# Eight single PSUM banks, gathered tails of M, and a new order in a two-block kernel

## The chip, the cores and the metric

The kernel runs on one core of one Trainium2 chip. A core has several engines with an instruction list each: TensorE (PE, matmuls, with its weight loads shown as PEld), VectorE (DVE), ScalarE (ACT), GpSimd (POOL) and SyncE (SP), which here issues all DMAs. An engine takes its own list in order and waits for others through semaphores. PE writes to PSUM alone, and DVE and ACT take results out of it ("evict" them) into SBUF.

The metric is the time of one launch on the device in microseconds (us), lower is better. The span of a profile is the time from the first to the last instruction; the launch's own time is a little longer.

## The reference

Two blocks that share nothing are computed and set side by side in the last dimension. Block A is a long convolution over the sequence (S = 2048, D = 576) by FFT, with a short convolution and gates around it. Block B is linear attention with 32 heads of 18 columns.

```python
# A: k_shift = sum over 4 taps of k_pad[:, t:t+S] * shift_k;  kv = k_shift * v
kv_f = rfft(kv_pad);  kf_f = rfft(kf_pad)          # length 2 * S
y = irfft(kv_f * kf_f)[:S].astype(bf16)
a = q * (y + kv * ssm_D)

# B: q, k, v = split of x @ wqkv into 32 heads of 18 columns
phi = lambda t: where(t > 0, t + 1, exp(t)) + 1e-6
kv = einsum("bhsd,bhse->bhde", phi(k), v);  z = einsum("bhsd->bhd", phi(k))
num = einsum("bhqd,bhde->bhqe", phi(q), kv)
den = einsum("bhqd,bhd->bhq", phi(q), z)[..., None] + 1e-6
b = (num / den) merged @ wo

out = concatenate([a, b], axis=-1)
```

## The kernel before

Every piece of work is a small function, called a unit, and the string ORDER lists the units one after another. A scheduler is not at work: each engine gets its instructions in the order in which the units are written. A unit's name is followed by its arguments, by letters that say which engine does its vector work (A for ACT, D for DVE, P for POOL, N for "not done, the matmuls of the next stage take both summands"), and after a slash by digits that name the buffers it takes.

Block A's 576 channels go in five chunks: four of 128 and one of 64. For each chunk the filter (h) and the gated input (u) pass the same stages:

- hT turns the filter's rows (on PE, or through a copy and a transposing DMA), and cv makes u by the short convolution in at, one multiply and one multiply-add pair per tap.
- h1 and u1 (L536) are the first half of the transform: matmuls with the matrix G, evicted into Ch and Cu. G is computed in the kernel by index arithmetic on DVE (ix) and a sine on ACT (sin).
- ht and ut transpose Ch and Cu by DMA into Cth and Ctu (L543), each in two halves.
- h2 and u2 (L559) are the second half, evicted into T and SU.
- pX and pT multiply SU with T into X and T, pA and pS add or subtract their two planes.
- i1 (L593) and i2 (L606, L607) are the inverse; i2 reads F, the transposed G, which FT makes by a transposing DMA (L613), and multiplies its result into q.

Block B computes k and q (k, q, qt; L455, L464) with an exponential on ACT and a combination on DVE (phi). It forms G = x' * phi(k) (L661), kv from it and the weights of v, M = kv * wo (b_M, L712 to L719), the denominators (den), their reciprocals, and bc and bt, which spread the reciprocals over the heads and multiply them into phi(q) (pqT and pq4). The output units o and ol multiply pqT and pq4 by M (L783, L775) and send the rows out.

PSUM is given out in four slots of two banks each: a unit's tile takes a whole slot, however small it is. M has 576 columns, more than a bank holds in 32-bit numbers, so each of M's five units makes 512 columns and then 64, evicted together. The denominators' unit also makes a column that carries the epsilon (ez) in the same slot.

The two memsets that set the bias row of the weights wqk (one_w, unit wm) stand behind the first evictions on DVE.

## Time and profile before

| What | us |
|---|---|
| launch, median of 3 runs | 161.46 |
| launch, lowest and highest of the 3 | 159.47, 189.46 |
| launch of the profiled execution | 159.33 |
| its span | 157.6 |

Mean granted PE clock over the profiled execution: 0.989 of full speed. Section 2 of the page cuts the span into 40 slices; each digit is the busy share of a slice in tenths:

```profile
PE   7999999999998999999999999999899999999991
DVE  6989779898999699997999998999998998899810
ACT  4999999999987899959999757998997969796141
POOL 6048703709113963008100049289998050230000
PEclk9999999999999999999999999999987999999999
```

PE is at nine tenths or more in nearly every slice, DVE and ACT in most. In a row of the timeline the columns are the start, the duration, the engine, the line, the operation with what it writes and reads, and in brackets how long the engine was idle before it and what ended that.

### The profile page before, as it was taken

The page shows a single profiled execution, that of the slowest core. Times are in us where ns is not written, and L with a number is a line of the kernel's source. Part 1 is how long each engine was busy: PE and PEld are TensorE (multiplying, and loading weights), DVE is VectorE, ACT ScalarE, POOL GpSimd, SP SyncE. Part 2 cuts the span into 40 slices and gives each one's busy share as a digit, 9 for nine tenths or more (in the row PEclk, how much of TensorE's full clock was granted, in tenths as well). Part 3 has the DMA queues.
Part 4 walks back from the last instruction along what each step waited for, and adds up shares of the span by engine and source line. Part 5 has one row for each costly group of instructions (what it writes and reads, how often), then busy time and mean ns, then how long its engine had stood idle before and what let it go on. Part 6 is the DMA issues. An engine that isn't in the chain of part 4 may idle for free.

```text
span 157.6 us, 4600 instructions
## 1 busy us (share of the span) xinstructions
PE 149.6 (95%) x1986; PEld 90.3 (57%) x1986; DVE 135.8 (86%) x169; ACT 130.5 (83%) x162; POOL 62.0 (39%) x70
## 2 busy tenths in 40 slices
PE   7999999999998999999999999999899999999991
PEld 2686555467533467367566468585445565578650
DVE  6989779898999699997999998999998998899810
ACT  4999999999987899959999757998997969796141
POOL 6048703709113963008100049289998050230000
PEclk9999999999999999999999999999987999999999
DMA  3986999999999699999999787697987999636076
GB/s 86 391 282 188 294 300 186 253 290 266 184 186 225 127 317 264 143 213 324 177 176 176 209 109 144 192 141 146 263 170 148 131 319 186 173 107 189 0 227 198
DMA packets 74315, 31.92 MB, mean 203 GB/s; under 512 B 52090, under 2 KB 73653, under 8 KB 74294
## 3 DMA queue, kind: packets, MB, share of 16 engines
q1 hardware_dynamic: 74294, 31.62, 91.5%
q8 instruction: 15, 0.25, 0.6%
q14 instruction: 6, 0.05, 0.1%
HBM read 14.97 MB, written 4.72 MB: 125 GB/s over the span
## 4 chain that ended last, share of the span: by engine, by line
PE 77%; ACT 12%; DMA 3%; DVE 3%; issue 1%; POOL 1%; DVEq 0%; POOLq 0%; ACTq 0%
PE k_ps L455 12%; PE g_ps L661 10%; PE o_ps L783 9%; PE s_ps L536 8%; PE q_ps L464 8%; PE i_ps L593 6%; PE s_ps L559 5%; DMA Ctu<-Cu 3%; PE i_ps L606 3%; PE i_ps L607 2%; ACT V L308 2%; ACT T L308 2%; ACT Cu L308 2%; PE o_ps L775 2%; ACT G L231 2%; PE qt_ps L472 2%
## 5 line engine op out<-in xcount | busy, mean ns | idle before, releaser
L455 PE MATMUL k_ps<-wqk,xT 128*128 128x512 bf16 (+1 forms) x160 | 21.5, 286 | 0.0
L536 PEld LDWEIGHTS <-G 128*128 128x128 bf16 x320 | 17.4, 98 | 3.6 <-issue 2.7
L464 PE MATMUL q_ps<-xT,wqk 128*128 128x512 bf16 x80 | 18.4, 380 | 0.0
L308 ACT ACTIVATE Cu<-s_ps 128x1024 bf16<-128x1024 f32 (+1 forms) x18 | 17.0, 976 | 0.4 <-PE s_ps L536 0.2
L455 PEld LDWEIGHTS <-xT 128*128 128x128 bf16 x160 | 11.4, 98 | 10.5 <-issue 0.3
L308 ACT ACTIVATE T<-s_ps 128x1024 bf16<-128x1024 f32 x17 | 16.8, 1026 | 0.6 <-PE s_ps L559 0.6
L308 ACT ACTIVATE ob<-o_ps 128x576 bf16<-128x576 f32 (+1 forms) x15 | 9.2, 637 | 9.1 <-PE o_ps L775 4.8
L661 PE MATMUL g_ps<-pk,x_sb 128*128 128x512 bf16 (+1 forms) x128 | 16.5, 286 | 0.0
L308 ACT ACTIVATE Ch<-s_ps 128x1024 bf16<-128x1024 f32 (+1 forms) x17 | 15.2, 928 | 1.0 <-PE s_ps L536 1.0
L494 DVE TENSOR_TENSOR at<-at 128x2048 bf16<-128x2048 bf16 (+1 forms) x14 | 15.5, 1109 | 0.5
L308 ACT ACTIVATE SU<-s_ps 128x1024 bf16<-128x1024 f32 x15 | 15.0, 1040 | 1.0 <-PE s_ps L559 1.0
L308 ACT ACTIVATE V<-i_ps 128x1024 bf16<-128x1024 f32 x15 | 14.7, 1039 | 1.0 <-PE i_ps L593 1.0
L783 PE MATMUL o_ps<-wo_M,pqT 128*128 128x512 bf16 (+1 forms) x112 | 14.9, 286 | 0.0
L448 DVE SCALAR_TENSOR_TENSOR pk<-pk,k_ps 128x576 bf16<-128x576 bf16 x16 | 11.8, 751 | 3.4 <-ACT pk L447 3.3
L493 DVE TENSOR_TENSOR at<-k,Wj 128x2048 bf16<-128x2048 bf16 (+1 forms) x13 | 14.7, 1134 | 0.1
L661 PEld LDWEIGHTS <-x_sb 128*128 128x128 bf16 x128 | 8.4, 97 | 8.9 <-issue 1.2
L447 ACT ACTIVATE pk<-k_ps,neg 128x576 bf16<-128x576 f32 x16 | 11.6, 741 | 1.3 <-PE k_ps L455 0.9
L464 PEld LDWEIGHTS <-wqk 128*128 128x128 bf16 x80 | 7.4, 98 | 9.1 <-issue 1.3
L608 DVE TENSOR_TENSOR q<-i_ps,q 128x1024 bf16<-128x1024 f32 (+1 forms) x10 | 10.9, 1105 | 1.9 <-PE i_ps L607 1.8
L783 PEld LDWEIGHTS <-pqT 128*128 128x128 bf16 x112 | 7.5, 98 | 7.7 <-issue 0.9
L536 PE MATMUL s_ps<-hT,G 128*128 128x128 bf16 (+1 forms) x160 | 10.7, 216 | 1.0 <-ACT G L231 0.4
L593 PE MATMUL i_ps<-W,T 64*128 64x128 bf16 x160 | 11.3, 217 | 0.4 <-DVE pqT L753 0.4
(163 smaller groups left out, 336.0 us busy)
## 6 DMA issues: line engine op xcount, KB each, us to landing
x_sb<-in_B_x_dram SPq DMA_DIRECT2D x4, 576.0 KB, 6.6
h_sb<-in_A_ssm_k_dram SPq DMA_DIRECT2D x4, 512.0 KB, 6.1
out_dram<-ob SPq DMA_DIRECT2D x7, 288.0 KB, 5.3
k<-in_A_k_dram SPq DMA_DIRECT2D x1, 1280.0 KB
v<-in_A_v_dram SPq DMA_DIRECT2D x1, 1280.0 KB
q<-in_A_q_dram SPq DMA_DIRECT2D x1, 1280.0 KB
wqk<-in_B_wqkv_dram SPq DMA_DIRECT2D x2, 576.0 KB, 7.8
k<-in_A_k_dram SPq DMA_DIRECT2D x1, 1024.0 KB
```

Source lines behind the costliest of these rows:

```text
L308: nc.scalar.activation(out=out, in_=in_, func=ACT.Copy)
L447: nc.scalar.activation(out=out_ap, in_=ps_ap, func=ACT.Exp, bias=K.neg1[0:n, :])
L448: nc.vector.scalar_tensor_tensor(out=out_ap, in0=out_ap, scalar=1.0, in1=ps_ap, op0=ALU.min, op1=ALU.max)
L455: nc.tensor.matmul(ps[:, n0:n1], lhsT=xT[r // 4][:, t, rr * 128:(rr + 1) * 128], rhs=wqk[:, t, D + n0:D + n1], start=(t == 0), stop=(t == 4))
L464: nc.tensor.matmul(ps[:, j, :], lhsT=wqk[:, t, 128 * c:128 * c + 128], rhs=xT[g][:, t, :], start=(t == 0), stop=(t == 4))
L493: on[0].tensor_tensor(out=t_, in0=kk[:, 3 - stage:19 - stage], in1=wb(stage), op=ALU.mult)
L494: on[1].tensor_tensor(out=a_, in0=a_, in1=t_, op=ALU.add)
L536: nc.tensor.matmul(ps[:, bi, 0:dc], lhsT=K.G[ri][:, b, :], rhs=xf(b), start=True, stop=True)
L593: nc.tensor.matmul(ps[:, r, g, :], lhsT=s[key, hf][64 * r:64 * r + 64, z, x, 128 * g:128 * g + 128], rhs=K.W[64 * r:64 * r + 64, m, :], st ...
L608: nc.vector.tensor_tensor(out=qs, in0=ps[:, :, 0:dc], in1=qs, op=ALU.mult)
L661: nc.tensor.matmul(ps[:, n0:n1], lhsT=x_sb[:, r, f0:f0 + fn], rhs=pk[:, r, n0:n1], start=(r == 0), stop=(r == 15))
L783: nc.tensor.matmul(pss[i][:, n0:n1], lhsT=pqT[:, c, r * 128:(r + 1) * 128], rhs=B['M'][:, c, n0:n1], start=(c == 0 and not first), stop=(c ...
```

## The change

PSUM becomes one tile of eight banks of 512 32-bit columns, and the digits in the order name a bank; a tile takes the banks that its size needs, from that one on. The tiles of the last, narrow chunk are made as wide as they are, so that they fit one bank.

M is split: b_M makes 512 columns in one bank, and a new unit Mt makes the 64 last columns of all five parts in another, with one eviction. The epsilon column of the denominators gets a unit of its own, ez, in a bank of its own, right behind zz.

```diff
+    allps = pspool.tile([128, 4096], FP32, name="allps")
     class Banks:
         def tile(self, shape, dt, name):
-            return pspool.tile(shape, dt, name=name, tag="ps" + slots.pop(0))
+            o = 512 * int(slots.pop(0))
+            v = allps[:, o:o + n // 2].bitcast(BF) if dt == BF else allps[:, o:o + n]
...
-        ps = psum.tile([128, 8, 128], FP32, name="s1_ps")
+        ps = psum.tile([128, 8, dc], FP32, name="s1_ps")
...
+    def m_mul(ps, c, n0, n1):
+        h0, hn = HCH[c]
+        if c < 4:
+            nc.tensor.matmul(ps, lhsT=B['kvT'][0:hn, c, :], rhs=B['wo'][0:hn, c, n0:n1], start=True, stop=False)
+            m = HCH[c + 1][1]
+            nc.tensor.matmul(ps, lhsT=B['kvx'][0:m, c, :], rhs=B['wo'][0:m, c + 1, n0:n1], start=False, stop=True)
...
     def b_M(c, eng='A'):
-        ps = psum.tile([128, 1024], FP32, name="m_ps")
-        for n0, n1 in ((0, 512), (512, 576)):
...
-        evict(B['M'][:, c, :], ps[:, 0:D], eng)
+        ps = psum.tile([128, 512], FP32, name="m_ps")
+        m_mul(ps[:], c, 0, 512)
+        evict(B['M'][:, c, 0:512], ps[:], eng)
+
+    def b_Mt(eng='A'):
+        ps = psum.tile([128, 5, 64], FP32, name="m_ps")
+        for c in range(5):
+            m_mul(ps[:, c, :], c, 512, 576)
+        evict(B['M'][:, :, 512:576], ps[:], eng)
+
+    def b_ez():
+        ps = psum.tile([128, 2], FP32, name="ez_ps")
...
+        ez = B['ez'] = ab.tile([128, 1], FP32, name="ez")
+        nc.vector.tensor_scalar_add(out=ez[:], in0=ps[:, 0:1], scalar1=EPS)
...
     def b_den():
-        ps = psum.tile([128, 1024], FP32, name="den_ps")
+        ps = psum.tile([128, 512], FP32, name="den_ps")
...
-        ez = ab.tile([128, 1], FP32, name="ez")
-        nc.vector.tensor_scalar_add(out=ez[:], in0=ps[:, 512:513], scalar1=EPS)
-        den = ps[:, 0:512]
+        ez = B['ez']
+        den = ps[:]
...
-io ls ix.0.0/0 sin.1.0 wu.1.A/0 wu.2.B/1 dl ix.1.0/1 sin.0.0 hl.0/0 dc/2 hd.0 Wj.A/301 ix.0.1 id xl.2 iw ix.1.1 sin.0.1
+io wm wu.1.A/0 ix.0.0/0 xl.2 sin.1.0 wu.2.B/1 dl ix.1.0/1 sin.0.0 dc/2 ls ix.0.1 ix.1.1 id sin.1.1 hl.0/0 hd.0 iw
```

Apart from that the whole order is new. Most units stay near their place; some change engine. In the rows below a name left of the arrow is what is written, and behind it what is read; in the changed kernel every PSUM tile reads as allps, and line numbers are ten to twenty higher.

At the head of DVE's list before (sm holds small constants, mp and mc the indices of the sines):

```order
L135 MEMSET epsc 128x1
L381 MEMSET sm 1x64
L148 TENSOR_SCALAR sm<-sm 128x128
L150 TENSOR_SCALAR mp<-sm 128x128
L153 TENSOR_TENSOR mp<-mp,sm 128x128
```

and in the changed kernel, at the same place:

```order
L135 MEMSET epsc 128x1
L371 MEMSET wqk 64x576
L372 MEMSET wqk 1x576
L148 TENSOR_SCALAR sm<-sm 128x128
L150 TENSOR_SCALAR mp<-sm 128x128
```

The two memsets of wqk have moved ahead of the first index operation.

DVE between kv and the last product of pqT before (Ch, SU, T are evictions or products of block A, at the short convolution, Gz holds the reciprocals):

```order
L310 CAST SU<-s_ps 128x2x512
L573 TENSOR_TENSOR T<-SU,T 128x2048
L493 TENSOR_TENSOR at<-k,Wj 128x16x64
L494 TENSOR_TENSOR at<-at 128x16x64
L739 TENSOR_SCALAR ez<-den_ps 128x1
L741 TENSOR_SCALAR den_ps<-den_ps,ez 128x512
L743 RECIPROCAL Gz<-den_ps 128x512
L608 TENSOR_TENSOR q<-i_ps,q 128x8x128 x2
L753 SCALAR_TENSOR_TENSOR pqT<-pqT,bc_ps 128x1024 x2
L762 SCALAR_TENSOR_TENSOR pq_77<-pq_77,bt_ps 128x1024
L310 CAST T<-s_ps 128x2x512
L753 SCALAR_TENSOR_TENSOR pqT<-pqT,bc_ps 128x1024 x6
```

and in the changed kernel:

```order
L320 CAST SU<-allps 128x2x512
L501 TENSOR_TENSOR at<-k,Wj 128x16x64
L583 TENSOR_TENSOR T<-SU,T 128x2048
L761 TENSOR_SCALAR allps<-allps,ez 128x512
L763 RECIPROCAL Gz<-allps 128x512
L618 TENSOR_TENSOR q<-allps,q 128x8x128 x2
L773 SCALAR_TENSOR_TENSOR pqT<-pqT,allps 128x1024 x2
L782 SCALAR_TENSOR_TENSOR pq_78<-pq_78,allps 128x1024
L773 SCALAR_TENSOR_TENSOR pqT<-pqT,allps 128x1024 x2
L320 CAST Ch<-allps 128x2x16x16
L773 SCALAR_TENSOR_TENSOR pqT<-pqT,allps 128x1024 x4
```

A multiply and an add of the convolution, the eviction of T and ez have left this stretch; the first step of the last convolution and a half-width Ch have come into it.

SP's queue around the transposes of F before:

```order
L543 DMA_TRANSPOSE Cth<-Ch 128x16x128 x2
L613 DMA_TRANSPOSE F_1350<-G_107 128x16x128
L524 DMA_TRANSPOSE hT<-hp 128x16x128
L632 DMA wv_GT<-in_B_wqkv_dram 128x4x576
L634 DMA wv_GT<-in_B_wqkv_dram 64x576 x2
L543 DMA_TRANSPOSE Ctu<-Cu 128x16x128 x2
L646 DMA wo_M<-in_B_wo_dram 126x4x576
```

and in the changed kernel:

```order
L642 DMA wv_GT<-in_B_wqkv_dram 128x4x576
L644 DMA wv_GT<-in_B_wqkv_dram 64x576 x2
L553 DMA_TRANSPOSE Cth<-Ch 128x16x128 x2
L534 DMA_TRANSPOSE hT<-hp 128x16x128
L623 DMA_TRANSPOSE F_1509<-G_126 128x16x128
L623 DMA_TRANSPOSE F_1511<-G_114 128x16x128
L553 DMA_TRANSPOSE Ctu<-Cu 128x16x128 x2
L656 DMA wo_M<-in_B_wo_dram 126x4x576
```

Both transposes of F now stand behind hT and right ahead of Ctu; one of them came from a place between the first two Ctu transposes, much earlier, and the loads of the weights of v have moved ahead of Cth.

## The prediction

> **What bounds the kernel now.** I read the page's busy times first, then the two stretches into which the trace divides around 122 us, then the timelines of the engines where PE (TensorE) loses time. In the windows the columns are busy time and instruction count of PE, PEld, DVE, ACT and POOL, then granted clock, DMA share and GB/s.

> ```profile
> span 157.6 us, 4600 instructions
> PE 149.6 (95%) x1986; PEld 90.3 (57%) x1986; DVE 135.8 (86%) x169; ACT 130.5 (83%) x162; POOL 62.0 (39%) x70
> 98.00:122.00 24.00, 22.26 (x404) 13.58 (x405) 23.02 (x22) 22.07 (x29) 20.02 (x7) 0.93 0.86 175
> 122.00:154.00 32.00, 31.76 (x475) 19.57 (x469) 25.77 (x29) 21.90 (x30) 4.25 (x2) 1.00 0.71 168
> 114.00:116.00 2.00, 1.68 (x34) 1.07 (x32) 2.00 (x3) 2.00 (x4) 2.00 (x2) 1.00 0.81 161
> 116.00:118.00 2.00, 1.98 (x25) 0.90 (x18) 2.00 (x3) 1.84 (x3) 2.00 (x2) 0.71 0.95 196
> 118.00:120.00 2.00, 2.00 (x24) 0.66 (x22) 1.31 (x2) 1.25 (x3) 2.00 (x2) 0.50 1.11 210
> 120.00:122.00 2.00, 1.64 (x60) 1.31 (x46) 2.00 (x3) 1.83 (x3) 1.38 (x1) 0.94 0.43 84
> ```

> PE is the bound: 149.6 of 157.6 us, and 31.76 of the last 32 us before the final output. A kernel that does the same matmuls can win only what PE loses. The largest loss stands between 98 and 122 us: 24.00 - 22.26 = 1.74 us idle, and a clock that fell to 0.71, 0.50 and 0.94, which costs 2 x (0.29 + 0.50 + 0.06) = 1.70 us of matmul rate. There DVE (VectorE) is busy for 23.02 of 24 us, more than PE. So in this stretch, the only one, I take DVE's list of work as what sets the pace; behind it PE does.

> The change keeps the matmuls of M, of the denominators and of everything else, moves them, and gives PSUM out in single banks. I go through it by the places where it touches a bound.

> **Start.** The memset pair that prepares wqk moves from its place among the evictions to the head of DVE's list, ahead of the index arithmetic on which the first sine waits.

> ```profile
> 1.28 0.29 DVE L148 TENSOR_SCALAR sm<-sm 128x128 int32<-128x128 f32 x1 [0.17 <-POOL sm L121]
> 5.41 0.28 DVE L69 TENSOR_SCALAR ident<-sm 128x128 bf16<-128x128 f32 x1
> 12.53 0.54 DVE L361 MEMSET wqk<- 64x576 int32 x1
> 13.71 0.57 DVE L207 TENSOR_SCALAR sm<-sm 128x448 int32<-128x448 int32 x1
> 3.62 1.15 ACT L231 ACTIVATE G<-mp,negpi 128x1024 bf16<-128x1024 int16 x1 [1.32 <-DVE sm L427]
> 4.00:8.00 4.00, 3.91 (x45) 2.62 (x44) 3.72 (x11) 3.97 (x7) 0.00 (x0) 1.00 1.05 392
> 8.00:12.00 4.00, 3.63 (x61) 3.35 (x59) 3.36 (x4) 4.00 (x8) 1.79 (x5) 1.00 0.78 267
> ```

> From the first of the pair (L361) to the row behind the second (L207) are 13.71 - 12.53 = 1.18 us. DVE would start it at about 1.0 us and come to L148 at 2.18 instead of 1.28: +0.9 us. The first sine, which waited 1.32 us for DVE, starts 0.9 us later, and ACT (ScalarE) has no slack to take it back: 3.97 of 4 and 4.00 of 4 us. The identity moves behind the second half of the indices too, to about 7.2 us, so PE's first transposes come later, but those wait for ACT's evictions in any case. I take +1.0 us on the first k matmuls. Bounds: 0 if ACT loses its small waits, +1.5 if PE's start follows the identity in full (7.2 - 5.41 = 1.8, less PE's wait for the sine).

> **The two DMA waits near 45 us.** PE waits twice there for a transposed copy of stage-one results.

> ```profile
> 42.01 0.62 PE L559 MATMUL s_ps<-Cth,W 64*32 64x512 bf16 x16 [0.34 <-DMA Cth<-Ch]
> 48.24 0.41 PE L559 MATMUL s_ps<-Ctu,W 64*32 64x512 bf16 x8 [0.52 <-DMA Ctu<-Cu]
> 43.02 2.17 SPq L543 DMA_TRANSPOSE Ctu<-Cu  x1
> 45.23 2.53 SPq L613 DMA_TRANSPOSE F<-G  x1
> 47.86 2.62 SPq L543 DMA_TRANSPOSE Ctu<-Cu  x1
> ```

> Together 0.86 us. SP's queue, not PE, sets when these land, and the same loads stand ahead of them, so a PE that comes 1.0 us later finds them there; besides, the 2.53 us transpose of F leaves the place between the two Ctu transposes. I take -0.8 (bounds -0.86 and 0, if SP slips as much as PE). Start and DMA waits together: +0.2. What is late next on SP is F itself; that is a rival below.

> **Extra matmuls.** One sum of two planes after another is left to the matmuls of the inverse stage (N in the order): pA of chunk 0, half 0 gets its addition on DVE (16 matmuls fewer), pS of chunk 1, half 1 and of chunk 2, half 0 lose theirs (32 more). Net 16.

> ```profile
> 72.59 2.12 PE i_ps L593 x72
> ```

> 2.12 / 72 = 29 ns each, so 0.47 us of PE. They add in full if PE is the bound where they stand; the second 16 stand just ahead of the output rows, at a place where PE waits for DVE now. I take +0.1 of it beyond that cover.

> **DVE between the denominators and the first output rows.** The first output unit starts when the last product of pqT and the spread reciprocals is done.

> ```profile
> 101.56 0.68 DVE L493 TENSOR_TENSOR at<-k,Wj 128x1024 bf16<-128x1024 bf16 x1
> 102.28 0.69 DVE L494 TENSOR_TENSOR at<-at 128x1024 bf16<-128x1024 bf16 x1
> 102.89 0.15 DVE L739 TENSOR_SCALAR ez<-den_ps 128x1 f32<-128x1 f32 x1
> 103.94 3.36 DVE L743 RECIPROCAL Gz<-den_ps 128x512 bf16<-128x512 f32 x1
> 113.01 1.23 DVE L310 CAST T<-s_ps 128x1024 bf16<-128x1024 f32 x1
> 119.51 2.35 DVE L753 SCALAR_TENSOR_TENSOR pqT<-pqT,bc_ps 128x1024 bf16<-128x1024 bf16 x2 [0.69 <-PE bc_ps L749]
> 93.07 0.68 DVE L491 TENSOR_TENSOR at<-k,Wj 128x1024 bf16<-128x1024 bf16 x1
> 127.97 0.69 DVE L310 CAST Cu<-s_ps 128x512 bf16<-128x512 f32 x1 [0.34 <-PE s_ps L536]
> 122.49 2.13 PE L783 MATMUL o_ps<-wo_M,pqT 128*128 128x512 bf16 x16
> ```

> From this list go the two convolution steps of the last chunk, to POOL (0.68 + 0.69), the eviction of one T, to ACT (1.23, whose successors start 1.14 after it), and ez (0.15), which moves to the place after zsel: -2.6. To it come the first convolution step (0.68, seen at 93.07) and one half-width Ch eviction (0.69 by the like eviction of Cu): +1.3. Net -1.3 us. The last products now start at 119.51 and end at 121.86, and PE's first long output matmuls stand at 122.49. The 0.69 us for which DVE waits on bc_ps falls in the slow-clock time; I give half of it, 0.3, to the finer banks: M, den, ez and the half-width tiles hold one bank and not two, so bc finds a free pair sooner. That makes -1.6. Bounds of this term: 0, if PE and not DVE sets the pace, and -3.4, if all idle time and all clock loss (1.74 + 1.70) go.

> POOL's cover: its queue has the two convolution steps (2.14 us each by POOL's own convolution row) in the 3.3 us that it waits for SU now, and gets rid of three X sums. If they came late, the next to wait would be X and T of chunk 2 and then the inverse stage, behind POOL's 20.02 of 24 us.

> ```profile
> 117.16 2.14 POOL L493 TENSOR_TENSOR at<-k,Wj 128x1024 bf16<-128x1024 bf16 x1
> 102.89 4.06 POOL L571 TENSOR_TENSOR X<-SU,T 128x2048 bf16<-128x2048 bf16 x1 [3.28 <-ACT SU L308]
> 105.35 1.24 ACT L308 ACTIVATE wo_M<-m_ps 128x576 bf16<-128x576 f32 x2
> ```

> The tails of M: five evictions of 576 columns become five of 512 and one of 320. At 0.62 us each, and nearly the same per column, ACT gains or loses some 0.3 us of fixed cost; ACT idles 24.00 - 22.07 = 1.93 us there. I take 0, bounds 0 and +0.3.

> [...] By the three rows, time at half clock was 1.70 x 2 = 3.4 us, after 2 us in which PE idled 0.32. [...] I keep one such dip in the sum.

> **After 122 us.** PE's matmuls there are the same, 31.76 busy of 32. DVE gets two X sums and two output evictions more and one convolution step and one T product less, about +1.0 us, against 32 - 25.77 = 6.2 idle. Cover enough on the whole; I take +0.2 for single waits. The last eviction and its DMA are unchanged.

> **Sum.** +0.2 (start and DMA) + 0.1 (matmuls) - 1.6 (DVE) + 0.2 (end) = -1.1 us. The profiled execution took 159.33 us (span 157.6, the other 1.7 us lie around it and stay); so 158.2 us, 0.7% less. The median of the three runs shown is 161.46, with 159.47 below it and 189.46 above; the profiled one is at the low end, and a plain median may well lie 1% higher than the sum.

> **Rivals.**

> The F transposes come too late (slower). Both now go out on SP after hT of chunk 3, right ahead of the matmuls that read F, and two Ctu transposes queue behind them.

> ```profile
> 72.70 6.34 SPq L543 DMA_TRANSPOSE Cth<-Ch  x2
> 79.09 2.63 SPq L613 DMA_TRANSPOSE F<-G  x1
> 82.72 2.02 SPq L524 DMA_TRANSPOSE hT<-hp  x1
> 88.94 6.92 SPq L543 DMA_TRANSPOSE Ctu<-Cu  x2
> 53.77 5.54 SPq L543 DMA_TRANSPOSE Cth<-Ch  x1
> DMA to landing us min/median/max: 4.7/4.7/4.7
> 92.73 0.22 PE L606 MATMUL i_ps<-V,F 128*128 128x128 bf16 x1
> ```

> hT ends at 82.72 + 2.02 = 84.74; two F issues of 2.6 us end at 90, and the second lands 4.7 us after its start, at about 92.0; PE needs it at 92.73 plus 0.2 to 0.5. The margin is a microsecond. With issues of 5.54 us, as one transpose shows, the second starts at 90.3 and lands between 95.0 (4.7 us on) and 97.9 (if the landing stretches by the same 2.9 us). PE works in order and waits up to 4.9 us, and the Ctu transposes, at 95.8 instead of 88.94, come behind it: 159.33 - 1.1 + 4.9 = 163.1. PE waits from 93.0 on; slower by over 2% it is from a landing at 97.3 on. The 2.53 and 2.63 of both F rows and the 2.02 of hT speak against it. Chance 0.09.

> The banks and the order change nothing that counts (same). If PE sets the pace between 98 and 122 us, DVE's relief is idle time, and the 16 matmuls and part of the start stay: 159.33 + 0.2 + 0.5 + 0.2 = 160.2. For it: PE is busy 22.26 of 24. Against: 1.74 us idle with DVE full. [...] Chance 0.17.

> Both losses go (lower than forecast). PE fed without idle time and without a dip: 159.33 + 0.2 + 0.5 - 3.4 = 156.6. For it: the dip follows PE's idle slices; against: DVE still has over 21 of 24 us. Chance 0.19.

> My forecast, 0 to -2 us from the profiled time: chance 0.55.

> **Chances and range.** About 2% is what a measurement of this kernel tells from no change. 2% below the profiled time is 156.1, below the median 158.2; which of them the comparison starts from is open, so the low rival and a small part of the forecast count as faster: 0.26. Slower is the F rival without its mild end: 0.07. The rest, 0.67, is within 2%. The range leaves out the F rival's upper part and the extremes of the low one: 156.2 to 161.2, the top being the 160.2 of the second rival and 1 us for the spread that two of the runs show.

> **What would show it.** Start right: first sine near 4.5 us and first k matmuls near 14.0 (now 12.96). DMA: no PE waits of 0.3 us or more between 40 and 50. DVE: last bc products end near 120.5, first long output matmuls near 121.2. Wrong: a PE wait on F at 93 us; a clock dip at another place; a new wait on DVE's X sums after 122 us.

## The result, and the profile after

The changed kernel takes 161.28 us (median of 20 executions, 160.28 to 163.59), the kernel before 159.39 in the same comparison (20 executions): a ratio of 1.0154, 95% interval 1.0124 to 1.0185. The forecast was 158.2 us, a gain of 0.7%; it is a loss of 1.5%, inside the 2% line, and the median stands 0.1 us above the range's top of 161.2. Ratios leave disturbed executions out, medians do not, so the two can differ by up to 0.6%.

The busy times and the chain of work that ended last, on the page of the changed kernel, and then its two stretches around 122 us (busy time and count of PE, PEld, DVE, ACT and POOL, granted clock, DMA share, GB/s):

```profile
span 160.2 us, 4674 instructions
...
PE 149.9 (94%) x1985; PEld 92.3 (58%) x2002; DVE 136.2 (85%) x171; ACT 129.9 (81%) x161; POOL 63.9 (40%) x69
...
PE 60%; DMA 21%; ACT 7%; DVE 6%; issue 4%; SPq 0%; ACTq 0%; DVEq 0%
```

```profile
98.00:122.00 24.00, 22.01 (x400) 14.43 (x396) 22.79 (x28) 21.51 (x28) 22.90 (x8) 1.00 0.91 175
122.00:154.00 32.00, 30.40 (x513) 20.18 (x511) 26.67 (x31) 21.54 (x27) 7.47 (x3) 1.00 0.67 157
```

PE is busy as long as before, but in a longer span. The clock's dip of before near 117 us is not there, and the time is longer all the same. Of the 2.6 us by which the span is longer than the one before, 2.0 stand there at the first k already. The timeline of PE in the kernel before, then in the changed one (start, time, operation, count, and the idle time before it; W_ps are one-row matmuls that spread the weights of the short convolution, hT and xT transposes of the filter and of x):

```profile
1.06 3.65 PE L79 MATMUL warm_ps<-sm 128*128 128x512 bf16 x9 [1.06 <-DVE negpi L129]
...
4.78 1.13 PE L391 MATMUL W_ps<-pqT,sm 1*128 1x512 bf16 x5
5.92 1.16 PE L515 MATMUL hT_ps<-ident,h_sb 128*128 128x128 bf16 x16
...
12.96 6.39 PE L455 MATMUL k_ps<-wqk,xT 128*128 128x512 bf16 x50
```

```profile
1.06 4.02 PE L79 MATMUL allps<-sm 128*128 128x512 bf16 x9 [1.06 <-DVE negpi L129]
...
5.37 2.10 PE L401 MATMUL allps<-pqT,sm 1*128 1x512 bf16 x5
7.46 1.90 PE L525 MATMUL allps<-ident,h_sb 128*128 128x128 bf16 x16
9.16 1.68 PE L356 MATMUL allps<-ident,x_sb 128*128 128x128 bf16 x16
...
14.94 6.29 PE L465 MATMUL allps<-wqk,xT 128*128 128x512 bf16 x49
```

The five W_ps matmuls take 2.10 us instead of 1.13 (they start 427 ns apart instead of 215), the sixteen transposes of the filter 1.90 instead of 1.16 (106 ns apart instead of 62): TensorE (PE) is still slow, the W_ps at half the rate. The first k stands at 14.94 instead of 12.96 us. The row of the granted clock shows 1.00 there, but only because the record has no entry yet: its first entry, 1.00, is at 4.20 us before and at 10.46 us in the changed kernel.

### The profile page after: what moved, and what is told of

Its sections match the earlier page's. It is cut to its first block, busy times and chain, and to the rows that moved or that the text cites. A ratio compares the mean times of both kernels' runs of the same rounds, so it can differ in the third digit from the quotient of the medians.

```text
span 160.2 us, 4674 instructions
## 1 busy us (share of the span) xinstructions
PE 149.9 (94%) x1985; PEld 92.3 (58%) x2002; DVE 136.2 (85%) x171; ACT 129.9 (81%) x161; POOL 63.9 (40%) x69
## 4 chain that ended last, share of the span: by engine, by line
PE 60%; DMA 21%; ACT 7%; DVE 6%; issue 4%; SPq 0%; ACTq 0%; DVEq 0%
PE allps L465 10%; DMA Cth<-Ch 8%; PE allps L803 7%; DMA Ctu<-Cu 7%; PE allps L546 6%; DMA h_sb<-in_A_ssm_k_dram 6%; PE allps L474 5%; PE allps L671 5%; PE allps L569 4%; PE allps L603 4%; ACT Cu L318 3%; PE allps L525 3%; PE allps L616 2%; PE allps L617 2%; PE allps L482 1%
## 5 line engine op out<-in xcount | busy, mean ns | idle before, releaser
L465 PE MATMUL allps<-wqk,xT 128*128 128x64 bf16 (+1 forms) x154 | 20.9, 282 | 0.3
L318 ACT ACTIVATE Cu<-allps 128x1024 bf16<-128x1024 f32 (+1 forms) x18 | 16.9, 975 | 2.5 <-DMA Cth<-Ch 1.6
L474 PE MATMUL allps<-xT,wqk 128*128 128x512 bf16 x78 | 18.3, 380 | 0.1
L318 ACT ACTIVATE V<-allps 128x1024 bf16<-128x1024 f32 x15 | 14.9, 1030 | 4.0 <-DMA Ctu<-Cu 2.1
L318 ACT ACTIVATE T<-allps 128x1024 bf16<-128x1024 f32 x18 | 17.6, 1022 | 0.1
L671 PE MATMUL allps<-pk,x_sb 128*128 128x65 bf16 (+1 forms) x124 | 16.1, 283 | 0.3 <-issue 0.2
L318 ACT ACTIVATE Ch<-allps 128x1024 bf16<-128x1024 f32 (+1 forms) x16 | 14.5, 951 | 1.4 <-PE allps L546 1.4
L318 ACT ACTIVATE SU<-allps 128x1024 bf16<-128x1024 f32 x15 | 14.9, 1031 | 0.6 <-PE allps L569 0.5
L803 PE MATMUL allps<-wo_M,pqT 128*128 128x64 bf16 (+1 forms) x107 | 14.1, 282 | 0.9 <-issue 0.5
L458 DVE SCALAR_TENSOR_TENSOR pk<-pk,allps 128x576 bf16<-128x576 bf16 x16 | 11.8, 750 | 2.3 <-ACT pk L457 2.3
```

Of the source, the lines that this page charges most:

```text
L318: nc.scalar.activation(out=out, in_=in_, func=ACT.Copy)
L458: nc.vector.scalar_tensor_tensor(out=out_ap, in0=out_ap, scalar=1.0, in1=ps_ap, op0=ALU.min, op1=ALU.max)
L465: nc.tensor.matmul(ps[:, n0:n1], lhsT=xT[r // 4][:, t, rr * 128:(rr + 1) * 128], rhs=wqk[:, t, D + n0:D + n1], start=(t == 0), stop=(t == 4))
L474: nc.tensor.matmul(ps[:, j, :], lhsT=wqk[:, t, 128 * c:128 * c + 128], rhs=xT[g][:, t, :], start=(t == 0), stop=(t == 4))
L671: nc.tensor.matmul(ps[:, n0:n1], lhsT=x_sb[:, r, f0:f0 + fn], rhs=pk[:, r, n0:n1], start=(r == 0), stop=(r == 15))
L803: nc.tensor.matmul(pss[i][:, n0:n1], lhsT=pqT[:, c, r * 128:(r + 1) * 128], rhs=B['M'][:, c, n0:n1], start=(c == 0 and not first), stop=(c ...
```

## The experiments

All timings are against the kernel before on the same chip, in 6 to 12 executions each. The kernels are edited by moving units in the order. Where half of one order is joined to half of the other, the buffer digits are renamed to fit.

### Banks, and parts of the start

The order of before on the new eight-bank tile (all PSUM digits doubled):

> The order, the units of M and of the denominators as before the change; only PSUM is one tile of eight banks, and each slot number becomes a pair of banks. Theory start and rival late stretch alike: the way PSUM is given out costs nothing, ratio 0.998 to 1.002, the trace as before. Rival one tile (waits between units become stricter or looser when PSUM is one tile): ratio off by more than 0.004.

E3 gave 159.72 us, a ratio of 1.0014 (0.9970 to 1.0059). Within this interval the banks make no difference.

The memsets of wqk, moved back in the changed kernel, and moved to the front in the kernel before:

```diff
-io wm wu.1.A/0 ix.0.0/0 ...
+io wu.1.A/0 ix.0.0/0 ...
...
-... xd.2.DA/046 hT.1.D/02 sin.0.1 ...
+... xd.2.DA/046 hT.1.D/02 wm sin.0.1 ...
```

> The changed kernel with one unit moved: the wqk memsets stand behind the second filter transpose again, as before the change. Theory start (a late start is carried to the end): the first sine starts 0.9 us earlier than in the changed kernel and the first k matmuls 0.9 to 1.0 us earlier; ratio to the kernel before 1.0154 minus 0.006, so about 1.009. Rival DMA (the start is set by the order of the first loads and by the clock, not by DVE): first sine earlier, first k matmuls within 0.3 us of the changed kernel's, ratio 1.013 to 1.016. Rival late stretch (the loss comes from waits behind 85 us): ratio unchanged, 1.015.

> The kernel before, with one unit moved: the wqk memsets at the head of DVE's list. Theory start: first sine 0.9 us later, first k matmuls 0.9 us later, ratio 1.005 to 1.006. Rival DMA: first k matmuls within 0.3 us of before, ratio 0.999 to 1.002.

Back: 161.38 us, 1.0114 (1.0072 to 1.0156), a small gain at most. To the front of the kernel before: 159.64 us, 1.0048 (1.0011 to 1.0084), with the first k at 13.97 instead of 12.96 us. Alone, neither explains 1.5%.

The changed kernel with the first 38 units of before:

> The changed kernel, but all units up to the weights of k stand in the order that they had before the change (banks doubled to fit). Theory start: first k matmuls near 13.0 us as before, 2.0 us ahead of the changed kernel, and the gain is carried to the end: ratio 1.000 to 1.005. Rival late stretch: PE reaches the denominators 2 us earlier and loses it again in waits for Ctu and V; ratio 1.012 to 1.016.

It gave 162.43 us, 1.0192 (1.0136 to 1.0247): not better. PE's waits in this run (total, times, longest) name the reason:

```profile
PE allps L475 <- DMA wqk<-in_B_wqkv_dram: 1.0, 1, 1.0
...
PE allps L466 <- DVE xT L321: 0.6, 1, 0.6
...
PE allps L526 <- DMA h_sb<-in_A_ssm_k_dram: 0.3, 1, 0.3
```

The first k started early, at 13.39 us, and then waited for x and for the q part of wqk, which the new order loads behind k's data. Waits for Ctu (0.9 us) and Cth (0.7 us in two) come on top. That load order goes only with a late start, so the units up to k had to be exchanged as well.

### Longer pieces of the two orders

> As the run above, but only the units up to the third one behind the first k block (the load of k) stand as before: with them the loads of filter 2 and of wqk's q part go ahead of that of k, and the first two k blocks read the transposes of x that are there first. Where the start kept as before gave 162.4 us, since PE waited 0.27 and 0.65 us for transposes of x and 0.99 us for wqk, theory one (those three waits, and no other thing, ate the start's gain) expects the first q near 21.8 us, hT.2 near 38.4, no wait over 0.3 us between 12 and 27 us, and 159.3 to 159.9 us, a ratio of 0.998 to 1.004. Theory two (the order from 24 us on loses by itself) expects the first q near 21.8, but G.1 later than 66.9 us, and 160.4 us or more.

> The changed kernel, in which the order's units up to the third group of u2 of chunk 1 (about 67 us) stand as they did before, and all units behind it as the change has them. Theory one, the loss is made ahead of G and nowhere else: G.1 starts near 65.9 us in place of 67.97, first output tails near 122.0 in place of 124.03, and the end follows by the same 2 us: 159.2 us, a ratio to the kernel before of 0.995 to 1.002. Theory two, the loss is made again behind it, by the late V eviction that waits for a transpose and by the matmuls that the change adds: G.1 early, first tails near 122.8 and the time near 160.4 us, a ratio near 1.006.

> The order of before on eight banks, with the tails of M in one unit and the product with epsilon apart (behind zz), so with a lighter DVE list behind the denominators and nothing else of the new order. The forecast's step (DVE's list sets the time between the denominators and the first output rows, of which ez and its copy go: some 0.4 us here) expects 159.0 us, a ratio near 0.997. The theory that PE sets the pace there expects no difference that can be measured: 159.2 to 159.8 us, ratio 0.998 to 1.003, with DVE's idle time between 98 and 122 us longer by what was taken off it.

> As the run with the order of before, M's tails and epsilon apart, but from the second output block (about 122 us) on the units stand as the change has them. If the stretch behind 122 us loses by its own order (V of chunk 2 waiting for a transpose, PE idle some 1 us more of 32), the time is 0.5 us over that of the run with before's order: 159.9 us, ratio near 1.003. If that wait only comes from what is late ahead of it, the time is that of the run with before's order within 0.2 us and the V eviction waits less than 0.5 us.

E6 gave 159.59 us, 1.0050 (1.0016 to 1.0085): exchanging the start as far as k takes back about two thirds of the loss. Five of its six executions lie between 159.39 and 159.65 us; the sixth, the profiled one, took 162.23 us, and there the first entry of the clock's record stands at 13.14 us. The same program, then, loses 2.6 us in some executions.

The other three gave 161.62 (1.0178), 162.62 (1.0235) and 162.77 us (1.0235), which fits neither theory of theirs. The joined orders have faults of their own: in e7 and e8 the product with epsilon stands directly behind zsel and PE waits 0.5 us for it, and in e5 PE waits 0.9 us for an eviction of SU. E7's profile also has a late first entry (9.85 us) and a fall of the clock for 6.83 us from 119.1 us on. E8 lies 0.15 us from e7, on whose order it is built, well within the spread of the two. These three do not say what M's tails or the late part of the order cost by themselves; that stays open. In the profiles of e2 and e5 the clock rose early (4.76 and 4.39 us) and did not fall before the end, and they are slow all the same: what these joined orders lose there is not lost by the clock.

### The clock

> The changed kernel as it is. In the profile shown of it the record of the granted clock began at 10.5 us, with matmuls 106 ns apart before that and 62 ns behind, where the kernel before had 4.2 us; with before's first loads and units up to k, and all else as changed, one execution with a record from 13.1 us took 162.2 us and five others 159.4 to 159.7 us. Theory one (the order of the head loses through the clock: TensorE stays at half rate longer, or drops once more, in most executions): executions fall into groups, near 159.5 us where the mean clock is 1.00 and the start is fast, and 1.5 to 2.5 us above it where the clock fell for 3.4 us (a mean near 0.987) or the start was slow; a profile from the first group has the first k near 13.0 to 13.5 us. Theory two (the order loses by waits, whatever the clock): no execution below 160.2 us, and the first k at 14 us or later also where the record of the clock begins by 5 us.

> The changed kernel with four more warm-up matmuls ahead of the first real ones (13 in place of 9; at half rate they last until 6.8 us, where W_ps could start at 5.4 us). [...] Theory two, the start is set by loads and by DVE and not by PE: the warm-up is in the way of W_ps and the time rises by the 0.5 to 1.4 us that it is longer: 161.8 us or more.

> The kernel before on eight banks (159.7 us, a ratio of 1.001 to before), with the head of the new order alone: its first 38 units, up to where W is built (wqk's memsets first, the first load of x ahead of the filter's and D's, sines interleaved otherwise). Theory one, the head costs 1.7 us of the 2.5: a median of 160.8 to 161.4 us, ratio 1.010 to 1.015, and again more executions with a mean clock near 0.987 or a slow start than the kernel before has. Theory two, the head's delay is absorbed before G.1 as the forecast's upper bound had it (1.0 us or less is left): 159.2 to 160.2 us, ratio under 1.006.

> The changed kernel with before's units up to the first k blocks (which gave 159.6 us, a ratio of 1.005), and with the three sums whose place changed between PE and the other engines as before too: 16 matmuls fewer on PE (0.47 us), one difference on DVE, one on POOL. If PE is the engine that sets the end behind 66 us, the time falls by 0.3 to 0.5 us: 159.1 us, a ratio near 1.002. If DVE sets it between the denominators and the output (the forecast's step), it rises or stays: 159.6 us or more.

E10 is the largest effect of the study:

```diff
-    for _ in range({'A': 5, 'B': 4}[n]):
+    for _ in range({'A': 5, 'B': 8}[n]):
```

Four extra matmuls on zeros bring the changed kernel from 161.60 us (e9, 1.0166) to 159.54 us, 1.0036 (1.0001 to 1.0071). They delay W_ps to 6.57 us, and the first k still comes earlier than without them:

```profile
1.06 5.44 PE L80 MATMUL allps<-sm 128*128 128x512 bf16 x13 [1.06 <-DVE negpi L130]
...
6.57 1.13 PE L402 MATMUL allps<-pqT,sm 1*128 1x512 bf16 x5
7.63 1.22 PE L526 MATMUL allps<-ident,h_sb 128*128 128x128 bf16 x16
...
14.28 6.29 PE L466 MATMUL allps<-wqk,xT 128*128 128x512 bf16 x50
```

In e9's profile, with nine matmuls, the record begins at 12.74 us and the first k at 15.93. Its least time, 160.46 us, speaks rather for theory two of that run. A later execution of the same kernel (e16) took 159.86 us, but its clock rose late too, at 10.37 us, so it is not the fast start of theory one. E10 speaks against theory two: a longer warm-up and nothing else takes the loss away.

E12, the order of before with the new head alone, gave 161.92 us, 1.0188 (1.0139 to 1.0238): on the order of before, the head by itself makes a loss of this size.

E11 missed: 163.27 us, 1.0228 (1.0161 to 1.0295). Taking one sum off PE's matmuls and giving it to DVE made PE wait 1.2 us for DVE's T, and 1.74 us go at the first matmuls of a G block with no releaser in the trace, which I cannot explain. Its clock rose early (4.68 us) in this profile.

```profile
PE allps L672 <- issue: 1.7, 1, 1.7
PE allps L604 <- DVE T L587: 1.2, 1, 1.2
```

### Whether the clock of the start decides

> The kernel before with the warm-up of 13 matmuls in place of 9, and nothing else. In the profiled execution of the changed kernel with that warm-up the record of the clock began at 6.07 us and the first k stood at 14.28 us (before: 4.20 and 12.96). [...] Theory two (every order has the slow start as often, and the longer warm-up helps each by the same 2 us): 157.5 us or less, a ratio under 0.993.

> The changed kernel with before's units up to the first k blocks (159.6 us, ratio 1.005, with one execution of six at 162.2 us from a slow start), with the warm-up of 13 matmuls. Theory one (what the head of the new order loses, it loses by the clock at the start and by nothing else): the two remedies don't add up, the time is that of the changed kernel with the long warm-up or of this one without, 159.2 to 160.0 us, ratio 1.002 to 1.008, with no execution over 161 us. Theory two (the head also loses by its loads and its DVE list): the sum of both is better than either, 158.5 us or less.

> The changed kernel with two more warm-up matmuls (11; they end by 5.9 us at half rate, so 4.8 us of work in place of 4.0). [...] Theory two (the four extra matmuls helped in another way, by shifting the work against the loads): two of them give half of it in every execution, 160.5 us with all executions within 0.8 us.

> The changed kernel as it is, once more, for a profile of an execution whose mean clock is below 0.99 (7 of the first 20 had 0.984 to 0.988, against 2 in 49 of the kernel before and none in 12 with the longer warm-up). Theory one (the fall belongs to the start: a clock that rose with the warm-up falls again while W_ps, one row high, and the waits for loads leave TensorE little used): the record shows 0.5 between 5 and 15 us, and the first k comes 1.5 us or more later than 13 us. Theory two (the fall is the one before 122 us that the kernel before shows in its profile, at the two waits for reciprocals): 0.5 between 100 and 130 us, and a start that is fast. If the profile again falls on an execution without a fall, this stays open.

E13 gave 158.55 us, 1.0014 (0.9991 to 1.0037): the kernel before gains nothing on the median, though none of its twelve executions is above 159.2 us, where those with nine matmuls reach 161.2 beside them. E14 gave 159.32 us, 1.0077 (1.0046 to 1.0108): the two remedies do not add up, as theory one had it. E15, with eleven matmuls, gave 161.18 us, 1.0176 (1.0146 to 1.0206), above the 160.5 us of theory two: a smaller dose did not help. But its profile shows what the others had not. The start in windows, columns as above, then PE's timeline at the place:

```profile
4.50:7.90 3.40, 2.45 (x21) 1.18 (x20) 3.14 (x12) 3.40 (x6) 0.31 (x1) 1.00 1.01 368
7.90:11.30 3.40, 3.40 (x35) 3.40 (x34) 1.61 (x2) 2.33 (x6) 0.00 (x0) 0.50 0.82 278
11.30:15.00 3.70, 3.70 (x65) 3.60 (x64) 3.29 (x3) 3.70 (x5) 2.51 (x8) 1.00 0.37 87
```

```profile
5.37 1.14 PE L402 MATMUL allps<-pqT,sm 1*128 1x512 bf16 x5
7.46 1.64 PE L526 MATMUL allps<-ident,h_sb 128*128 128x128 bf16 x16 [0.95 <-DVE sm L190]
8.90 1.91 PE L357 MATMUL allps<-ident,x_sb 128*128 128x128 bf16 x16
```

The clock rose at 4.48 us, PE then had little but the one-row W_ps and 0.95 us of idle time, and the clock stood at 0.50 for 3.41 us, from 7.90 to 11.31 us. So the new head can lose in two ways: the clock rises late, or it rises and falls again.

E16 (161.33 us, 1.0180, interval 1.0132 to 1.0227) was to catch such a fall in the changed kernel itself; its profile fell on another late rise, so there the place of the fall is not seen. The counts in its expectation are wrong; the right ones stand in the next table. One fall to 0.50 for 3.41 us makes a mean clock of 1 - 0.5 x 3.41 / 160 = 0.989, so executions with a fall can be counted without looking at the record. (The clock also falls near the end, where PE has little left to do; in the twenty profiles that takes at most 0.0053 off the mean.)

```
kernel                              executions   mean clock < 0.99   median us
before (its runs in five batches)       93              12           158.3 to 158.8
changed kernel                          20              14           161.28
changed, again (e9, e16)                12               8           161.60, 161.33
changed, 11 warm-up matmuls (e15)        6               5           161.18
changed, 13 warm-up matmuls (e10)       12               0           159.54
before, 13 warm-up matmuls (e13)        12               0           158.55
before's start and k, 13 (e14)           8               0           159.32
changed, memsets back (e1)              12               6           161.38
before, memsets first (e4)              12               6           159.64
identity first, memsets back (e18)      12               2           159.29
```

The mean does not say where a fall stands. That those of the changed kernel stand in the start is argued from e15's profile and from their absence in e10; the six profiles of the new head, or most of it, with nine matmuls and the memsets or the identity still late (after, e1, e9, e12, e16, e17) all show a late rise, and none a fall. Nor does every fall cost 2 us: the six executions of e4 with one have a median of 159.8 us, the six without 159.6.

```
stretches of 3.41 us                          time with such matmuls     number
the clock rose at the end                     2.67 to 3.41 us            20
it did not rise                               0 to 2.58 us               36
the next stretch, clock stayed                2.00 us or more            19
the next stretch, clock fell (e15)            1.23 us                     1
```

The first two rows do not overlap, nor do the last two. Later stretches lie between the last two: one with 1.67 us (e11) kept the clock, and at the end one with 1.54 us (e15) lost it. These are counts in twenty executions; what decides in the hardware is not shown.

Nine warm-up matmuls last from 1.06 to 5.05 us. What follows is my estimate from the counts, with every position of the stretches taken as equally likely. A stretch has 2.67 us of the nine if it ends between 3.73 and 5.79 us, which is 2.06 of 3.41 us of all positions, 60%; else the clock would rise only with the transposes, at 10 to 13 us as in the profiles with a late rise. Thirteen last until 6.4 us or later and would give some stretch 2.67 us at any position. If the clock does rise early, the next stretch matters too: in nineteen profiles it had 2.00 us or more, in e15 1.23. In the kernel before, hT.0 starts at 5.92 us and that stretch has 2.13 us; in the changed one it starts at 7.46, and a stretch beginning at 4.5 us would have (5.05 - 4.5) + (7.91 - 7.46) = 1.0 us. So the changed kernel should have a bad start in nearly every execution, 60% by a fall and the rest by a late rise: 14 of 20 had a fall. The same estimate asks more of the kernel before than the runs show. Its head has the same nine matmuls, so the clock should rise late in about 40% of its executions, and only 18 of the 93 are above 160 us. Either the positions are not evenly spread, or a late rise often costs less than 2 us.

The start differs between executions: the same head has its first entry at 4.93 us in e3 and at 9.85 us in e7. The remedies of the start are worth 161.4 - 159.4 = 2.0 us, 1.2% (the changed kernel against e10, and e18 below), and the order of units decides who pays.

### Which units of the head

```diff
-io wm wu.1.A/0 ix.0.0/0 xl.2 sin.1.0 wu.2.B/1 dl ix.1.0/1 sin.0.0 dc/2 ls ix.0.1 ix.1.1 id sin.1.1 hl.0/0 hd.0 ...
+io ls wm wu.1.A/0 ix.0.0/0 sin.1.0 wu.2.B/1 dl ix.1.0/1 sin.0.0 dc/2 id ix.0.1 ix.1.1 sin.1.1 hl.0/0 xl.2 hd.0 ...
```

> The changed kernel with three units of its head put forward again: the loads of the shift row and its memset right behind the first constants, the identity on DVE ahead of the second half of the DFT index (one operation of 0.28 us, which stood at 7.04 us in the profile with 11 warm-up matmuls, where the clock rose at 4.48, TensorE then idled 0.95 us in front of hT.0, and the clock fell to 0.5 from 7.90 to 11.31), and the first load of x behind that of the filter. wqk's memsets stay at the head of DVE. Theory one (the fall and the slow start come from the little used TensorE between the warm-up and hT.0): hT.0 starts by 6.8 us with no wait over 0.3 us ahead of it, executions with a mean clock of 0.984 to 0.989 become few, the median is 159.6 to 160.6 us, a ratio of 1.006 to 1.013. Theory two (that gap is not what matters): the mean clock is below 0.99 in half of the executions as before and the median 161 us or more.

> As the run above, with wqk's memsets put back behind the second filter's transposes as well, so that DVE's list ahead of the identity is 1.1 us shorter and hT.0 can start near 6.0 us as before. Theory one: no gap in front of hT.0, no execution with a mean clock below 0.99 in the start, slow starts as rare as before: 159.2 to 160.0 us, ratio 1.003 to 1.009, as the changed kernel with the longer warm-up (159.5 us) or with before's units up to k (159.6 us). Theory two: 161 us or more, as with the memsets put back alone (161.4 us).

E17 gave 161.45 us, 1.0187 (1.0134 to 1.0240), theory two's time: with wqk's memsets still at DVE's head it does not help, and four of its six executions have a fall. E18, the same with the memsets back, gave 159.29 us, 1.0032 (1.0004 to 1.0060), where the memsets alone (e1) had given 161.38. Each edit alone does little, both together nearly all. E18's start:

```profile
5.17 1.34 PE L402 MATMUL allps<-pqT,sm 1*128 1x512 bf16 x5
6.43 1.22 PE L526 MATMUL allps<-ident,h_sb 128*128 128x128 bf16 x16
...
14.05 1.24 PE L466 MATMUL allps<-wqk,xT 128*128 128x512 bf16 x5 [0.66 <-DVE Ch L321]
```

Its twelve executions fall into eight from 158.37 to 159.34 us and four from 160.85 to 161.96: a late rise or a fall still comes, but less often. What held e17 back in an execution whose clock rises early was not seen, since its profile fell on a late rise. No version beat the kernel before; e3 and e13 equal it.

## Why the forecast was wrong, step by step

**Start, +1.0 us: the mechanism right as far as it went, the size too small.** The first sine stands at 4.45 us (forecast 4.5). The memsets alone, in the kernel before, put the first k at 13.97 us (e4), as forecast 14.0; in the changed kernel with a clock that rises early (6.07 us) it stands at 14.28 us (e10). But the forecast counted the later identity only as PE's waiting, with 1.5 us as the bound, and put the clock of the start at nothing. The new head lets the clock rise late or fall again, and the first k came at 14.8 to 15.9 us in four profiles with nine matmuls, wqk's memsets first and the changed body (after, e9, e16, e17): +1.9 to +3.0 instead of +1.0. This is the step that failed: mending the start takes 2.0 us off the median, by e10 and by e18. How a late clock becomes 2.0 us is shown only in part. Between the profiles of the changed kernel and of e10 the first k makes 0.7 us of 2.4; 1.2 more are lost by the time of the first Ctu matmuls near 50 us (see the two DMA waits below), and most of the rest behind 122 us.

**One dip kept in the sum: the wrong place.** The forecast weighed the clock only where the profile showed it low, near 117 us, and not at the start, where its rows show 1.00; the record of the changed kernel begins at 10.46 us. The changed kernel's profile has no dip near 117 us; of the kernel before only 12 of 93 executions have a fall at all.

**The two DMA waits, -0.8 us: did not come in the shown profile.** There the forecast's other bound (0, if SP slips as much as PE) holds; PE's timeline of the changed kernel, then SP's:

```profile
44.24 0.62 PE L569 MATMUL allps<-Cth,W 64*32 64x512 bf16 x16 [0.40 <-DMA Cth<-Ch]
...
50.41 0.62 PE L569 MATMUL allps<-Ctu,W 64*32 64x512 bf16 x16 [0.47 <-DMA Ctu<-Cu]
```

```profile
40.05 3.63 SPq L349 DMA_TRANSPOSE xT<-in_B_x_dram  x1
```

The load of x's transposes that stands ahead of Ctu on SP went out at 38.53 us before and at 40.05 now. This differs between executions. In e16, the same kernel with the first k at 14.90 us and a clock that rose as late, PE waits at neither place:

```profile
43.42 0.63 PE L569 MATMUL allps<-Cth,W 64*32 64x512 bf16 x16
...
49.26 0.62 PE L569 MATMUL allps<-Ctu,W 64*32 64x512 bf16 x16
```

It is 1.15 us ahead there and took 159.86 us, against 161.90. E10 does not wait either, and e18 waits 0.23 us; there the saving came. E9, e15 and e17 wait 1.1 to 1.5 us. Where PE waits (after, e9, e15, e17) SP's first two transposes of Ch take 8.4 to 8.8 us, in e1, e10, e16 and e18 7.1 to 7.3. So a late clock does not force these waits; whether the longer warm-up keeps them away, or its one profile escaped them, is not shown.

**Extra matmuls, +0.1 beyond cover: mis-sized.** From the first G to the denominators e3 takes 34.73 us, and e16, e10 and e18 take 35.21, 35.29 and 35.42, all without a fall there: +0.5 to +0.7, where the matmuls are 0.47, so nothing seems to have covered them. E11, which undid them, was worse for other reasons, so this is a difference of profiles and not an isolated cost.

**DVE's list, -1.6 us: mostly idle time.** The timeline of DVE from the denominators to the last product, first in the order of before on banks (e3), then in the changed kernel:

```profile
102.20 0.76 DVE L752 TENSOR_SCALAR allps<-allps,ez 128x512 f32<-128x512 f32 x1
103.00 3.36 DVE L754 RECIPROCAL Gz<-allps 128x512 bf16<-128x512 f32 x1
106.27 2.29 DVE L619 TENSOR_TENSOR q<-allps,q 128x1024 bf16<-128x1024 f32 x2
...
112.27 1.22 DVE L321 CAST T<-allps 128x1024 bf16<-128x1024 f32 x1 [0.32 <-PE allps L570]
113.42 7.09 DVE L764 SCALAR_TENSOR_TENSOR pqT<-pqT,allps 128x1024 bf16<-128x1024 bf16 x6
```

```profile
104.75 0.76 DVE L761 TENSOR_SCALAR allps<-allps,ez 128x512 f32<-128x512 f32 x1 [0.18 <-PE allps L569]
105.54 3.36 DVE L763 RECIPROCAL Gz<-allps 128x512 bf16<-128x512 f32 x1
109.29 1.23 DVE L618 TENSOR_TENSOR q<-allps,q 128x1024 bf16<-128x1024 f32 x1 [0.39 <-PE allps L617]
111.11 1.23 DVE L618 TENSOR_TENSOR q<-allps,q 128x1024 bf16<-128x1024 f32 x1 [0.59 <-ACT T L318]
...
117.99 0.69 DVE L320 CAST Ch<-allps 128x512 bf16<-128x512 f32 x1
118.67 4.62 DVE L773 SCALAR_TENSOR_TENSOR pqT<-pqT,allps 128x1024 bf16<-128x1024 bf16 x4
```

The convolution steps and ez that left stood ahead of the denominators, where DVE now waits 0.18 us for PE: they bought idle time. Behind it the T of 1.22 us gave way to a Ch of 0.69, a gain of 0.53, but DVE now waits 0.39 and 0.59 us for PE and ACT, against 0.32 before. From the denominators' start to the end of the last product are 18.54 us, against 18.31 in e3. So the second rival (PE sets the pace, DVE's relief is idle) was right here. No run measures the 0.3 us for the finer banks in the new order. M's tails have no separate measurement.

**After 122 us, +0.2: too low in the shown profile.** PE is busy 30.40 of 32 us, against 31.76. ACT's eviction of V, and PE behind it, waited for Ctu: V of one chunk takes the buffer that a transpose of Cu still reads. ACT's timeline, then PE's:

```profile
126.13 1.94 ACT L318 ACTIVATE V<-allps 128x1024 bf16<-128x1024 f32 x2 [2.13 <-DMA Ctu<-Cu]
```

```profile
127.21 0.23 PE L603 MATMUL allps<-W,T 64*128 64x128 bf16 x2 [0.68 <-ACT V L318]
```

With the same units PE is busy 31.83 of 32 us in e18, and 31.86 in e16, whose clock rose late and where V does not wait; in e10, whose clock rose early, V waits 2.19 us and PE is busy 31.37. So this loss does not hang on the late clock; what brings it on stays open.

**The F rival** did not occur: PE has no wait for F in the profile.

Together: with the start mended, the changed kernel stands 0.3% (e18, e10) to 0.8% (e14) above the kernel before, near the forecast's second rival. The rest, 0.7 to 1.2%, comes and goes with the start and its warm-up.

## What to carry to other kernels

The length of a warm-up is worth a measurement. Here nine warm-up matmuls (4.0 us) under the new head gave 161.28 to 161.60 us, eleven 161.18 and thirteen (5.4 us) 159.54, and with thirteen none of the 32 executions of e10, e13 and e14 has a mean clock below 0.99. By my estimate from the counts above, 2 x 2.67 = 5.3 us in one piece would do at any position. What stands behind the warm-up matters as well: in e15 the one-row W_ps and 0.95 us of idle time came behind the early rise, and the clock fell. Work moved ahead of the first matmuls can therefore cost more than its own time: the memsets put the first k 1.0 us later (e4), and the whole new head took the order of before from a ratio of 1.0014 (e3) to 1.0188 (e12). A profile of one execution shows one start; the spread and the mean clock of some ten executions show what it costs. Relief of an engine is worth something only behind the last event that the engine itself decides, here the denominators' end on PE.

## What the hardware showed that was not expected

- The record of the granted clock says nothing of the time ahead of its first entry (10.46 us in the changed kernel), and the views show 1.00 there: the transposes of the filter are 106 ns apart in the changed kernel, 62 ns in the kernel before.
- A stretch full of work was not always followed by a rise: in e12 the 3.41 us from 6.08 to 9.49 us were full, 1.4 us of it W_ps on one row, and the clock did not rise. In e17 it rose at the end of the 3.41 us from 7.05 to 10.46 us, which hold hardly anything but transposes through PE.
- The counts of the start do not carry over to the middle: before the fall at 116.84 us in the kernel before, PE was busy for 2.88 of 3.41 us, though partly with matmuls on 32 and 64 rows, and before the fall at 119.08 us in e7 for 2.73. What decides there stays open.
